# Attention norm and gated conv FFN on one core: the norm factor of batches 6 and 7 spread by transfers through DRAM, three additions made by accumulating transfers, and a new order list

## The chip, the core and the metric

One core of a Trainium2 chip runs the whole kernel. Five engines work side by side, each through its own queue in order: TensorE (PE, matmuls; PEld is its weight load), VectorE (DVE), ScalarE (ACT), GpSimd (POOL) and SyncE (SP). SP does no arithmetic here; it issues transfers. Work on one engine waits for another by semaphores. The metric is device microseconds (us) of one launch, the median of several runs; lower is better.

## The reference

```python
kv  = einsum('bhsd,bhse->bhde', k, v)            # 8 batches, 8 heads, 576 rows, head size 64
out = einsum('bhsd,bhde->bhse', q, kv)
rms = sqrt(mean(out * out, axis=-1, keepdims=True) + 1e-06)
x   = (out / rms * g_norm)  -> (8, 576, 512)     # heads side by side
h   = maximum(x @ w_in, 0.0)                     # 512 -> 1024
conv = conv_w[0] * h[s-1] + conv_w[1] * h[s] + conv_w[2] * h[s+1]
y   = (h * sigmoid(conv)) @ w_out                # 1024 -> 512
```

Inputs and the output are float32; the kernel computes with bfloat16 operands and float32 sums.

## The kernel before

Features stand on the 128 partitions and sequence positions along the free axis. A batch's 512 features of x are four blocks `t` of 128 (two heads each); `u` is a pair of blocks, `s` one of two parts of the 576 positions (320 and 256 wide for batches 6 and 7, 256 and 320 for batch 0, 288 and 288 else). The 1024 features of h are eight blocks `f`, taken in four pairs `j`.

**The order is a list.** `ORDER` is a text of 852 tokens. A token such as `sp.6.1.1.6@6` calls the function `sp` with the arguments 6, 1, 1, 6; what stands behind `@` are buffer numbers (a PSUM bank, a slot of a ring). The program is issued in this order, and a loop at the end binds each engine's instructions to it. So the list fixes what each engine does one after the other, and a token that waits holds everything behind it on its own engine, and nothing on another engine unless that needs its result.

**The steps of a batch**, by token: `Lq`, `Lk`, `Lv` (L347) load from DRAM on POOL's queue with a cast. `kv` or `kz` (L402, L479) form the 64x64 products of k and v, `kva` or `kvd` copy them out of PSUM on ACT (L416) or DVE (L414). `qt` (L433) with `qd`, or a transposing transfer `tq` (L467), turn q. `ot` or `ox` (L460, L500) make the attention output in PSUM; `sq` (L509) squares it on ACT. Batches 0 to 3 then sum the squares over a head with `on` or `oq` (L528, L537), take the factor with `nl` (L545) and scale with `mo` (L556). Batches 4 and 5, and batches 6 and 7, are normed two at a time:

- `oc` (L521, ACT) copies the attention output out of PSUM in float32.
- `ss` (L566, PE) sums the squares of both batches into one PSUM tile of 128 rows, 32 per block `t`, one row per head, part and batch; it needs all `sq` of the batch.
- `ln` (L574, ACT) takes the reciprocal root, in float32. It needs a table load on ACT when sigmoids ran before.
- `sl` (L581 to L584, DVE, four instructions) splits that tile into bfloat16 parts.
- `sp` (L593, PE, two matmuls) spreads the rows of one batch, `u` and `s` over the 64 partitions of each head, into PSUM. There are eight for a pair of batches.
- `mu` (L599, DVE) multiplies: output copy by g_norm by the spread factor, into x.

Then `hm` or `hs` (L613, L628, PE) multiply x by w_in, and `re` or `rh` (L619, L640, ACT) take the positive part into h. `hs` of part `s` needs the `mu` of both `u` of that part. For a pair `j` of features, `ta` (L681, L682, DVE, two scalings, twice) writes the two outer taps, `aa` (L687, DVE) adds them, `ab` (L692, DVE) adds h, `sg` (L698, ACT) takes the sigmoid in place, and `mg` (L722, DVE) multiplies h by it. Batches 2 to 5 do this for two batches in one instruction (2304 elements), the others for one. Two tap buffers are used in turn.

`om` (L732, PE) multiplies h by w_out, 128 rows of a pair of batches at a time, in two halves of four matmuls; `ea` (L738, ACT) or `ed` (L743, DVE) copies the 128x512 result into a ring of rows, and `st` (L748, SP) stores it. `fi` (L286) are matmuls on zeros.

Of the kernel before, what the change touches and what calls it, by code (L numbers as in the profile page):

```python
# [54 lines left out]
AL = mybir.AluOpType  # L55
# [9 lines left out]
sq.0.1.1@3 oq.0.0.1@0 nl.0.0.1@2 fi.1.512@4 fi.1.512@4 hk.0.1.0.0@4 hk.0.1.0.1 rp.1.0@0 on.0.1.1@0 nl.0.1.1@3
hk.0.2.0.0@5 hk.0.2.0.1 rp.2.0 dg.3 mo.0.0.1 dg.2 hk.0.3.0.0@4 hk.0.3.0.1 hk.0.0.0.0@2 hk.0.0.0.1 rp.0.0 hk.0.0.1.0@3
rp.3.0 hk.0.1.1.0@5 hk.0.3.1.0@0 mo.0.1.1 hk.0.3.1.1 rp.3.1 hk.0.1.1.1 rp.1.1 hk.0.0.1.1 rp.0.1 dg.0 hk.0.2.1.0@1
hk.0.2.1.1 qt.1.0.0@6 kv.1.0.1@4 rp.2.1 cv.0.2@2 sc.0.2@0 cv.0.3@0 qd.1.0.0@2 kvd.1.0.1@1 ot.1.0.1@6 sc.0.3 pl
sq.1.0.1@4 cv.0.1@4 cv.0.0@2 Lq.1.2.2 Lk.1.2.2 Lv.1.2.2 sc.0.1@1 fi.2.512@0 qt.1.1.0@0 qd.1.1.0@3 mg.0.1.1 Lo.0.8
sc.0.0 mg.0.1.0 oq.1.0.1@4 nl.1.0.1@4 mo.1.0.1@1 fi.1.512@2 hk.0.5.1.0@2 hk.0.5.0.0@3 hk.0.5.0.1 rp.5.0 hk.0.5.1.1  # L70
rp.5.1 ta.0.1.5@0 hk.0.4.1.0@0 hk.0.4.1.1 rp.4.1 hk.0.7.0.0@1 hk.0.7.0.1 kv.1.1.1@4 kvd.1.1.1 rp.7.0 ot.1.0.0@2
sq.1.0.0@5 hk.0.7.1.0@6 hk.0.7.1.1 rp.7.1 ta.0.1.7@1 ot.1.1.1@0 sq.1.1.1@6 oq.1.0.0@4 nl.1.0.0@5 mo.1.0.0 hk.0.4.0.0@6
hk.0.4.0.1 rp.4.0 hk.0.6.1.0@7 hk.0.6.1.1 rp.6.1 oq.1.1.1@4 nl.1.1.1@6 mo.1.1.1 hk.0.6.0.0@6 Lq.2.0.4@2 hk.0.6.0.1
rp.6.0 ta.0.1.4 hk.1.6.1.0@7 ta.0.1.6 hk.1.0.1.0@2 ot.1.1.0@4 sq.1.1.0@7 aa.0.1.2 hk.1.1.1.0@3 hk.1.2.1.0@6 hk.1.6.1.1
rh.1.6.1 hk.1.1.1.1 rh.1.1.1 on.1.1.0@0 nl.1.1.0@7 mo.1.1.0 hk.1.2.1.1 hk.1.5.1.0@7 hk.1.5.1.1 rh.1.5.1 rh.1.2.1
hk.1.3.1.0@3 hk.1.3.1.1 rh.1.3.1 hk.1.0.1.1 rh.1.0.1 ab.0.1.2 sg.0.1.5 sg.0.1.4 qt.2.1.0@0 qt.2.0.0@6 hk.1.5.0.0@3
hk.1.5.0.1 rh.1.5.0 qd.2.0.0@4 hk.1.0.0.0@2 hk.1.4.1.0@4 hk.1.4.1.1 hk.1.0.0.1 hk.1.1.0.0@5 hk.1.6.0.0@6 hk.1.1.0.1
hk.1.2.0.0@7 hk.1.2.0.1 rh.1.2.0 rh.1.1.0 rh.1.0.0 hk.1.6.0.1 rh.1.6.0 aa.0.1.3 qd.2.1.0@0 ab.0.1.3 sg.0.1.7 sg.0.1.6
hk.1.7.0.0@0 mg.0.1.2 hk.1.7.1.0@1 hk.1.7.1.1 rh.1.7.1 hk.1.7.0.1 rh.1.7.0 ta.1.1.1@0 ta.1.1.0 Lk.2.0.4@1 Lv.2.0.4@0
Lq.3.0.4@0 Lk.3.0.4@0 Lv.3.0.4@1 Lq.4.0.4@1 aa.1.1.0 hk.1.4.0.0@3 om.0.1.0.4@2 rh.1.4.1 hk.1.4.0.1 rh.1.4.0  # L80
om.0.2.0.4@5 kv.2.0.2@6 mg.0.1.3 om.0.1.4.4 ab.1.1.0 sg.1.1.0 sg.1.1.1 kvd.2.0.2@2 ot.2.0.1@0 sq.2.0.1@0 ed.0.1@0
st.0.1 qt.3.1.0@6 qd.3.1.0@1 Lk.4.0.4@1 Lv.4.0.4@0 Lq.5.0.4@2 om.0.2.4.4 on.2.0.1@2 qt.3.0.0@6 qd.3.0.0@2 nl.2.0.1@8
mo.2.0.1@2 om.0.3.0.4@4 ea.0.2@1 ot.2.1.1@6 ot.2.1.0@2 mg.1.1.0 om.0.3.4.4 ed.0.3@2 sq.2.1.0@1 sq.2.1.1@2 on.2.1.0@0
nl.2.1.0@9 mo.2.1.0 om.0.0.0.4@5 hk.1.3.0.0@4 on.2.1.1@0 st.0.2 nl.2.1.1@0 mo.2.1.1 om.0.0.4.4 ed.0.0@3 ot.2.0.0@2
sq.2.0.0@3 hk.1.3.0.1 rh.1.3.0 st.0.0 kv.3.0.2@0 kvd.3.0.2@0 on.2.0.0@6 nl.2.0.0@1 mo.2.0.0 hs.2.0.1@4 rh.2.0.1@1
hs.2.5.1@5 rh.2.5.1 ot.3.1.1@0 sq.3.1.1@4 ta.1.1.5@1 ot.3.0.1@6 sq.3.0.1@5 hs.2.1.1@4 rh.2.1.1 hs.2.4.0@5 rh.2.4.0
# [52 lines left out]
def kernel(  # L139
# [685 lines left out]
```

## Time and profile before

| | |
|---|---|
| median of 3 runs | 177.66 us (177.49 to 177.71) |
| the profiled execution: its span | 175.6 us |
| PE / DVE / ACT / POOL busy | 167.9 / 149.5 / 148.9 / 22.2 us |
| `om`, L732: 512-wide matmuls | 62.8 us, 267 recorded |
| input product, L628 + L658 + L613 | 34.2 + 17.7 + 16.9 us |
| `sp`, L593: 32 matmuls | 3.4 us |
| `aa` on two batches, L687: 8 | 10.9 us |
| queue q0 (POOL's loads) | 14.50 MB, 49.2% of 16 engines' time |
| queue q1 (SP, ACT) | 13.11 MB, 26.2% |

The span is from the first to the last instruction of one profiled execution; the runs are timed from outside it. Busy time is the union of an engine's instructions. Matmuls are pipelined: a row of the PE timeline gives the start of a group and the time until its last matmul ends, so what a group costs is read from its start to the start of the next one. A group's mean in the list of groups is the time of one instruction from start to end; DVE and ACT instructions of one kind overlap by a little under 0.1 us. "Landing" is the time from the issue of a transfer until its semaphore tells that the data is there.

### The profile page before, as it was taken

What the parts mean: (1) busy time and instruction counts of PE and PEld (TensorE: products, weight loads), DVE (VectorE), ACT (ScalarE), POOL (GpSimd) and SP (SyncE); (2) the same over time, 40 slices, a digit from 0 to 9 for tenths busy, and PEclk for the clock granted to TensorE, in tenths of its full rate; (3) what the DMA queues carried; (4) which work ended last, traced back from release to release, by engine and by line L of the source; (5) the groups of instructions that cost most, each with busy time, mean ns of one, the idle gap of its engine ahead of it and who ended that gap; (6) DMA issues with size and microseconds to landing.
All of it is one profiled execution on the core that took longest, in us unless ns stands there. A gap on an engine that the chain in (4) does not pass through costs nothing.

```text
span 175.6 us, 5070 instructions
## 1 busy us (share of the span) xinstructions
PE 167.9 (96%) x2097; PEld 100.0 (57%) x2114; DVE 149.5 (85%) x290; ACT 148.9 (85%) x268; POOL 22.2 (13%) x35
## 2 busy tenths in 40 slices
PE   7979999999999999999999999999999999999992
PEld 2334766676447677644467764444877744444451
DVE  2796638899688899999999998989999999999950
ACT  2368899999978999999999998999999967676721
POOL 3094512200603013030000000000000000000000
PEclk9999999999999999999999999999999999999999
DMA  5999999999999999999999050330310003064486
GB/s 159 392 323 207 207 207 207 208 208 209 207 241 230 227 207 207 170 182 197 258 181 161 14 134 0 119 123 0 119 63 0 0 0 116 13 239 175 179 304 237
DMA packets 25911, 29.11 MB, mean 166 GB/s; under 512 B 6036, under 2 KB 20384, under 8 KB 25888
## 3 DMA queue, kind: packets, MB, share of 16 engines
q0 software_dynamic: 13296, 14.50, 49.2%
q1 hardware_dynamic: 12048, 13.11, 26.2%
q10 hardware_dynamic: 544, 1.18, 1.7%
q8 instruction: 16, 0.26, 0.6%
q14 instruction: 7, 0.06, 0.1%
HBM read 32.52 MB, written 9.44 MB: 239 GB/s over the span
## 4 chain that ended last, share of the span: by engine, by line
PE 76%; DVE 12%; ACT 5%; DMA 3%; issue 3%; ACTq 0%; DVEq 0%
PE banks L732 32%; PE banks L628 14%; PE banks L613 9%; PE banks L658 4%; DMA stg<-in_v_dram 3%; PE banks L460 3%; DVE h L722 2%; PE banks L708 2%; ACT taps L698 2%; PE banks L402 2%; PE banks L593 2%; PE banks L433 1%; PE banks L528 1%; DVE taps L681 1%; PE banks L286 1%
## 5 line engine op out<-in xcount | busy, mean ns | idle before, releaser
L732 PE MATMUL banks<-w_out_sb,h 128*128 128x512 bf16 x267 | 62.8, 379 | 1.2 <-issue 0.6
L698 ACT ACTIVATE taps<-taps,cw 128x576 bf16<-128x576 bf16 (+1 forms) x44 | 40.6, 958 | 5.7 <-DVE taps L692 5.5
L732 PEld LDWEIGHTS <-h 128*128 128x128 bf16 x280 | 26.2, 98 | 30.0 <-issue 1.1
L628 PE MATMUL banks<-x,w_in_sb 128*128 128x288 bf16 (+2 forms) x256 | 34.2, 286 | 0.0
L640 ACT ACTIVATE h<-banks 128x288 bf16<-128x288 f32 (+2 forms) x80 | 29.5, 460 | 0.3 <-PE banks L658 0.2
L628 PEld LDWEIGHTS <-w_in_sb 128*128 128x128 bf16 x256 | 24.4, 98 | 7.8 <-issue 0.8
L722 DVE TENSOR_TENSOR h<-h,taps 128x1152 bf16<-128x1152 bf16 (+1 forms) x24 | 22.8, 952 | 1.2 <-ACT taps L698 1.2
L687 DVE TENSOR_TENSOR taps<-taps 128x1152 bf16<-128x1152 bf16 (+1 forms) x22 | 21.5, 978 | 0.5
L509 ACT ACTIVATE sq<-banks 128x576 bf16<-128x576 f32 (+2 forms) x32 | 20.8, 691 | 1.1 <-PE banks L460 1.1
L692 DVE TENSOR_TENSOR taps<-taps,h 128x1152 bf16<-128x1152 bf16 (+1 forms) x22 | 21.4, 972 | 0.3
L681 DVE TENSOR_SCALAR taps<-h,cw 128x576 bf16<-128x576 bf16 (+1 forms) x44 | 18.7, 424 | 0.6 <-ACT h L665 0.5
L682 DVE TENSOR_SCALAR taps<-h,cw 128x576 bf16<-128x576 bf16 (+1 forms) x44 | 18.4, 418 | 0.0
L738 ACT ACTIVATE row<-banks 128x512 f32<-128x512 f32 x23 | 13.5, 597 | 5.7 <-PE banks L732 4.2
L658 PE MATMUL banks<-x,w_in_sb 128*128 128x288 bf16 (+2 forms) x128 | 17.7, 286 | 0.1
L613 PE MATMUL banks<-x,w_in_sb 128*128 128x288 bf16 x128 | 16.9, 286 | 0.0
L556 DVE SCALAR_TENSOR_TENSOR x<-banks,cw,rs 128x576 bf16<-128x576 f32 (+2 forms) x16 | 13.0, 816 | 3.9 <-ACT rs L545 3.6
L658 PEld LDWEIGHTS <-w_in_sb 128*128 128x128 bf16 x128 | 12.0, 98 | 4.4 <-issue 0.5
L227 ACT ACT_TABLE_LOAD x10 | 12.8, 1283 | 2.0 <-issue 1.8
L613 PEld LDWEIGHTS <-w_in_sb 128*128 128x128 bf16 x128 | 12.3, 98 | 3.7 <-issue 0.2
L443 DVE COPY qT<-banks 128x1152 bf16<-128x1152 bf16 (+2 forms) x13 | 8.8, 681 | 5.7 <-PE banks L433 5.7
L545 ACT ACTIVATE rs<-banks,eps_sb 128x576 f32<-128x576 f32 (+2 forms) x16 | 11.8, 740 | 1.1 <-PE banks L528 1.1
L599 DVE SCALAR_TENSOR_TENSOR x<-o,cw,banks 128x576 bf16<-128x576 f32 (+2 forms) x16 | 12.1, 810 | 0.7 <-PE banks L593 0.5
(89 smaller groups left out, 162.9 us busy)
## 6 DMA issues: line engine op xcount, KB each, us to landing
out_dram<-row SPq DMA_DIRECT2D x35, 256.0 KB, 2.3
q_sb<-in_q_dram POOLq DMA_DIRECT2D x6, 576.0 KB, 17.9
k_sb<-in_k_dram POOLq DMA_DIRECT2D x6, 576.0 KB, 14.5
v_sb<-in_v_dram POOLq DMA_DIRECT2D x6, 576.0 KB, 17.9
stg<-in_v_dram ACTq DMA_DIRECT2D x2, 576.0 KB, 6.2
stg<-in_k_dram SPq DMA_DIRECT2D x4, 288.0 KB, 6.9
w_in_sb<-in_moe_w_in_dram POOLq DMA_DIRECT2D x2, 512.0 KB, 9.9
w_out_sb<-in_moe_w_out_dram POOLq DMA_DIRECT2D x1, 1024.0 KB, 15.5
```

The lines of the kernel that those rows point to most:

```text
L509: nc.scalar.activation(T["sq", b, u, s], T["o", b, u, s], AX.Square)
L613: nc.tensor.matmul(ps[:, s, :HS], w_in_sb[:, t, f * P:(f + 1) * P], T["x", b][:, t, c0:c1], start=(t == 0), stop=(t == NT - 1))
L628: nc.tensor.matmul(ps, w_in_sb[:, t, f * P:(f + 1) * P], T["x", b][:, t, c0:c1], start=(t == 0), stop=(t == NT - 1))
L640: nc.scalar.activation(h, fr, AX.Relu)
L658: nc.tensor.matmul(T[at], w_in_sb[:, t, f * P:(f + 1) * P], T["x", b][:, t, c0:c1], start=(t == 0), stop=(t == NT - 1))
L681: nc.vector.tensor_scalar_mul(tap[:, 0, f % 2, :n, 8:8 + S], h[:, f], cw[:, f:f + 1])
L682: nc.vector.tensor_scalar_mul(tap[:, 1, f % 2, :n, :S], h[:, f], cw[:, 2 * NF + f:2 * NF + f + 1])
L687: nc.vector.tensor_add(tap[:, 1, :, :n, :S], tap[:, 0, :, :n, 7:7 + S], tap[:, 1, :, :n, 1:1 + S])
L692: nc.vector.tensor_add(y, y, span(b, n)[:, 2 * j:2 * j + 2])
L698: nc.scalar.activation(y, y, AX.Sigmoid, scale=cw[:, NF + f:NF + f + 1])
L722: nc.vector.tensor_mul(h, h, tap_of(b, j)[:, 1, :, :n, :S])
L732: nc.tensor.matmul(T["om", p, m], h[:, f, m * P:(m + 1) * P], w_out_sb[:, f, :], start=(f == 0), stop=(f == NF - 1))
```

## The change

1. **Norm factor of batches 6 and 7.** `sl.6` and the eight `sp.*.6` are gone. `dw.6` (one transfer on SP) stores the 128 x 320 float32 tile of `ln.6` to a DRAM scratch tensor. Eight `df` (two transfers each on SP, one for each head of a block) read one row per block back into all 64 partitions of a head, as a float32 tile in a buffer of q, k or v. `mu` reads that tile instead of PSUM. Batches 4 and 5 keep `sl` and `sp`.
2. **Three additions.** `aa.4.2.3`, `aa.4.2.0` and `aa.4.2.1` on DVE become `ad`, a transfer on POOL's queue from one tap row to the other that adds to what stands there (2 x 2 x 576 bfloat16 on each of 128 partitions). Its result stands in the other row, which `ab`, `sg` and `mg` then use; after `mg` DVE sets a column of zeros again that the sum has overwritten (four elements on each partition).
3. **A new list.** All 852 tokens are laid out anew. Apart from the two edits the counts per engine stay nearly the same: two kv copies go from DVE to ACT (`kvd` to `kva`, batches 2 and 3), one `oq` becomes `on`, seven row copies go from ACT to DVE (`ea` to `ed`: 1.0, 1.2, 1.3, 1.4, 1.8, 3.5, 3.6) and six the other way (2.8, 3.0, 3.2, 3.3, 3.4, 3.7). Buffer numbers change throughout. `on` and `oq` take one PSUM bank where both halves fit in it.

The code of it:

```diff
+    dram = pool("dram", 1, space=bass.MemoryType.DRAM)
...
+    def pair(n):
+        if 2 * n <= 512:
+            return bank()[:, :2 * n].rearrange("p (e n) -> p e n", e=2)
+        return bank2()[:, :, :n]
...
-        ps = T["on", b, u, s] = bank2()[:, :, :c1 - c0]
+        ps = T["on", b, u, s] = pair(c1 - c0)
...
     @op
+    def dw(b0):
+        T["rd", b0] = dram.tile([P, GW], FP32, name="rd")
+        nc.sync.dma_start(out=T["rd", b0], in_=T["rs", b0])
+
+    @op
+    def df(b, u, s, b0):
+        w, c = width(b, s), 2 * (b - b0) + s
+        to = T["sp", b, u, s] = ring("qkv"[(4 * (b - b0) + 2 * u + s) % 3], [P, 2, 320], FP32, "spread")[:, :, :w]
+        fr = T["rd", b0].rearrange("(t c i) w -> c i t w", t=NT, i=2)[c, :, 2 * u:2 * u + 2, :w]
+        for i in range(2):
+            nc.sync.dma_start(out=to[half(i)], in_=fr[i].unsqueeze(0).to_broadcast([D, 2, w]))
...
+    @op
+    def ad(b, n, j):
+        tap = tap_of(b, j)
+        T["y", b, j] = tap[:, 0, :, :n, 7:7 + S]
+        nc.gpsimd.dma_start(out=T["y", b, j], in_=tap[:, 1, :, :n, 1:1 + S], accum_op=AL.add)
+
+    def y_of(b, n, j):
+        if ("y", b, j) not in T:
+            T["y", b, j] = tap_of(b, j)[:, 1, :, :n, :S]
+        return T["y", b, j]
...
-        nc.vector.tensor_mul(h, h, tap_of(b, j)[:, 1, :, :n, :S])
+        nc.vector.tensor_mul(h, h, y_of(b, n, j))
+        if ADS & {(b, j)}:
+            nc.vector.memset(tap_of(b, j)[:, 0, :, :n, 7:8], 0.0)
```

The stretch of the list around the two edits, before:

```
... sq.7.1.0@7 oc.7.0.1@7 om.1.1.0.4@4 om.1.1.4.4 ss.6.6.2@5 ss.7.6.2 ln.6@0 oc.7.1.1@2 st.1.0 st.1.8 ea.1.1@4 oc.7.1.0@3
om.1.4.0.4@0 om.1.4.4.4 ea.1.4@2 om.1.7.0.4@1 ta.4.2.7@1 ta.4.2.6 aa.4.2.3 ab.4.2.3 om.1.7.4.4 ea.1.7@3 ta.4.2.5
aa.4.2.2 ab.4.2.2 sg.4.2.4 sg.4.2.5 sg.4.2.7 sl.6@1 sp.6.1.1.6@6 mu.6.1.1@0 sp.6.0.1.6@4 mu.6.0.1 sp.7.0.0.6@2
mu.7.0.0@2 st.1.2 st.0.5 om.1.5.0.4@0 om.1.5.4.4 sp.7.1.0.6@6 mu.7.1.0 sp.7.0.1.6@4 sp.7.1.1.6@2 om.1.3.0.4@1
om.1.3.4.4 ea.1.3@1 st.1.3 st.1.1 hs.7.6.0@6 rh.7.6.0@1 ...
```

and after:

```
... mg.2.2.3 ta.4.2.6 ta.4.2.4@1 om.1.2.4.4 om.1.8.4.4 kx.7@1 ed.1.2@0 sq.6.0.1@3 oc.6.0.1@3 ox.7.0.1@6 ox.7.1.1@0
ad.4.2.3 oc.7.0.0@4 sq.7.0.0@4 om.1.0.4.4 sq.7.0.1@5 oc.7.0.1@5 ox.7.1.0@2 om.1.3.0.4@6 ta.4.2.5 ed.1.8@1 sq.7.1.1@6
ss.6.6.2@4 sq.7.1.0@7 ss.7.6.2 ln.6@0 ed.1.0@2 aa.4.2.2 ab.4.2.2 om.1.3.4.4 ed.1.3@3 om.1.4.0.4@5 om.1.4.4.4
om.1.1.0.4@4 sg.4.2.5 sg.4.2.4 st.1.8 st.1.0 st.1.2 ab.4.2.3 dw.6 st.1.3 df.6.1.1.6@0 ed.1.4@0 df.6.0.1.6@0 mg.4.2.2
ta.4.2.1@1 sg.4.2.6 ta.4.2.0 oc.7.1.0@6 sg.4.2.7 mg.4.2.3 om.1.1.4.4 om.1.7.0.4@5 om.1.7.4.4 ea.1.7@1 ea.1.1@2
oc.7.1.1@7 om.1.5.0.4@6 om.1.5.4.4 mu.6.1.1@0 hm.4.3@2 ea.1.5@3 re.4.3 hm.4.2@4 om.1.6.0.4@0 re.4.2 om.1.6.4.4
df.7.1.0.6@1 mu.6.0.1 hs.6.5.1@1 hs.6.3.1@2 ta.4.2.3@0 ta.4.2.2 hs.6.7.1@3 hs.6.0.1@4 ea.1.6@4 df.7.0.0.6@1
hs.6.6.1@0 mu.7.1.0@1 mu.7.0.0 hs.6.1.1@5 hs.6.2.1@6 hs.7.2.0@7 ad.4.2.0 ab.4.2.0 ... mu.6.1.0 ... mu.6.0.0 ...
ad.4.2.1 ... mu.7.1.1 ... mg.4.2.0 ... ab.4.2.1 ...
```

The list's end, after the last gate product: before, `mg.7.1.2` is followed on PE by five halves and four whole row tiles of pair 3 and by two `oh`; after, by

```
mg.7.1.2 om.3.5.4.4 ed.3.5@1 om.3.7.4.4 ea.3.0@2 st.2.5 st.3.2 ea.3.7@0 om.3.6.0.4@2 st.3.0 om.3.6.4.4 st.3.7 st.3.5 oh.3.8.0@0
ed.3.6@2 eh.3.8.0@3 st.3.6 sh.3.8.0 om.3.4.0.4@1 om.3.4.4.4 ea.3.4@0 st.3.4 oh.3.8.1@0 eh.3.8.1@1 sh.3.8.1
```

where `oh` is half a row tile (256 wide), copied by `eh` and stored by `sh`.

More of the change, by code (lines that the diff above doesn't have):

```diff
@@ L65 @@
[L65 to L74, printed above, removed]
@@ L228, in act_table @@
                 {"rs": "abs_reciprocal_sqrt_and_small", "sig": "sigmoid_and_others"}[which])
+    ADS = {tuple(int(a) for a in tok.split("@")[0].split(".")[1::2]) for tok in ORDER.split() if tok.startswith("ad.")}
     TQ = {int(tok.split("@")[0].split(".")[1]) for tok in ORDER.split() if tok.startswith("tq.")}
@@ L286, in fi, with ff @@
             nc.tensor.matmul(ps[:, :w], zero[:, :P], zero[:, :w], start=True, stop=True)
+    @op
+    def ff(n, w):
+        ps, z = bank(), zero.bitcast(FP32)
+        for _ in range(n):
+            nc.tensor.matmul(ps[:, :w], z[:, :P], z[:, :w], start=True, stop=True)
     @op
@@ L408, in kvc @@
     def kvc(eng, b, u0, n):
-        if u0 == 0:
+        if ("kvb", b) not in T:
             T["kvb", b] = ring("kvb", [P, 2, 2 * D], BF16, "kvb")
@@ L437, in qc @@
     def qc(eng, b, u, s):
-        if s == 0:
+        if ("qT", b, u) not in T:
             T["qT", b, u] = ring("qT", [P, 2, S], BF16, "qT")
@@ L584, in sl, with h_of @@
         nc.vector.scalar_tensor_tensor(w, hi, nb[:, 0:1], r, op0=AL.mult, op1=AL.add)
+    @op
+    def dw(b0):
+        T["rd", b0] = dram.tile([P, GW], FP32, name="rd")
+        nc.sync.dma_start(out=T["rd", b0], in_=T["rs", b0])
+    @op
+    def df(b, u, s, b0):
[4 more added lines that the diff above has]
+            nc.sync.dma_start(out=to[half(i)], in_=fr[i].unsqueeze(0).to_broadcast([D, 2, w]))
+    def h_of(b, f):
+        if ("h", b // 2) not in T:
+            T["h", b // 2] = ring("h", [P, NF, 2, S], BF16, "h")
+        return T["h", b // 2][:, f, b % 2, :]
     @op
```

146 lines of the change are left out of this document (78 added, 68 removed).

## The prediction

> **What bounds the kernel now.** I read the page first, then the busy time by stretches of 20 us.
>
> ```profile
> span 175.6 us, 5070 instructions
> PE 167.9 (96%) x2097; PEld 100.0 (57%) x2114; DVE 149.5 (85%) x290; ACT 148.9 (85%) x268; POOL 22.2 (13%) x35
> PE 76%; DVE 12%; ACT 5%; DMA 3%; issue 3%; ACTq 0%; DVEq 0%
> ```
>
> ```profile
> 60.00:80.00 20.00, 19.75 (x392) 12.61 (x385) 19.64 (x36) 19.93 (x43) 3.70 (x5) 1.00 1.25 191
> ...
> 100.00:120.00 20.00, 19.70 (x138) 10.10 (x139) 18.29 (x26) 19.46 (x31) 0.00 (x0) 1.00 0.28 84
> 120.00:140.00 20.00, 19.86 (x158) 14.38 (x156) 19.55 (x28) 19.85 (x38) 0.00 (x0) 1.00 0.11 40
> ```
>
> The columns after the length are busy PE, PEld, DVE, ACT, POOL, then granted clock, DMA share and GB/s. TensorE (PE) is the bound, and VectorE (DVE) and ScalarE (ACT) are nearly as full: between 60 and 140 us all three run at 91 to almost 100%. So an edit that only frees DVE buys nothing by itself, and one that frees PE is paid only where ACT can follow. The chain of waits in the second half shows that PE runs without holes:
>
> ```profile
> 97.33 3.05 PE banks L613 x24
> ...
> 141.35 10.74 PE banks L732 x49
> ```
>
> That gives prices on the path: 0.219 us for one 512-wide matmul of the output product (L732), 0.127 for one 288-wide matmul of the input product (L613).
>
> **What leaves PE.** The eight spread products of batches 6 and 7 (L593) in the PE timeline:
>
> ```profile
> 113.96 0.68 PE L566 MATMUL banks<-sq,sel 128*32 128x320 bf16 x16
> 114.56 3.63 PE L732 MATMUL banks<-w_out_sb,h 128*128 128x512 bf16 x15
> 118.22 0.42 PE L593 MATMUL banks<-wparts,spread 32*128 32x256 bf16 x6
> 118.58 1.90 PE L732 MATMUL banks<-w_out_sb,h 128*128 128x512 bf16 x8
> 120.41 0.74 PE L593 MATMUL banks<-wparts,spread 32*128 32x320 bf16 x6
> 121.08 1.90 PE L732 MATMUL banks<-w_out_sb,h 128*128 128x512 bf16 x8
> ...
> 129.67 0.31 PE L593 MATMUL banks<-wparts,spread 32*128 32x320 bf16 x4
> 129.91 2.35 PE L628 MATMUL banks<-x,w_in_sb 128*128 128x320 bf16 x18
> ```
>
> From start to the next group's start they hold PE for 0.36 + 0.67 + 0.24 = **1.27 us**, not for sixteen full matmuls, since the short ones run side by side. That is all that PE gains; the rest of its work is the same, in another order (`on` for `oq` in one place: two 288-wide matmuls for four half ones that ran in pairs).
>
> **Where the new order can lose it.** PE is in order, and it meets ACT at the second `ss` (L566), which needs the last square of batch 7. In the new list two output tiles (16 matmuls) stand behind `ss` instead of ahead of it, and half a tile (4) ahead: 12 x 0.219 = 2.63 us less before, as much more behind. ACT ahead of that square:
>
> ```profile
> L738 ACT ACTIVATE row<-banks 128x512 f32<-128x512 f32 x23 | 13.5, 597 | 5.7 <-PE banks L732 4.2 <-issue 1.4
> L416 ACT ACTIVATE kvb<-banks 128x128 bf16<-128x128 f32 x2 | 0.6, 278 | 2.8 <-PE banks L402 2.8
> ```
>
> ```profile
> 112.26 1.68 ACT L509 ACTIVATE sq<-banks 128x512 bf16<-128x512 f32 x3
> ...
> 114.45 1.28 ACT L227 ACT_TABLE_LOAD   x1
> 115.74 0.53 ACT L574 ACTIVATE rs<-banks,eps_sb 128x320 f32<-128x320 f32 x1
> ```
>
> Four row copies go to DVE (4 x 0.597); one `oc`, the same kind of copy (0.6), and two copies of kv come in. The 256-wide kv copy on ACT is in no row; twice the 128-wide row is the top, the row itself the bottom (0.28 to 0.56), and I take 0.4: ACT has 2.39 - 0.6 - 0.8 = 0.99 us less ahead of the square. In the old run the squares ended at 113.94, as `ss` ran. So `ss` can come 0.99 us earlier if ACT stays as dense, and 2.63 if ACT loses no time at all. The end moves by that, plus the 2.63 moved behind, less 1.27: between +0.37 and -1.27. ACT stood idle for 1.8 us in this stretch, and the two kv copies fall near it:
>
> ```profile
> 42.00:60.00 18.00, 17.68 (x367) 10.90 (x368) 14.42 (x29) 16.20 (x33) 4.46 (x6) 1.00 1.19 226
> ```
>
> Half of that regained puts `ss` 1.9 us earlier and the end **0.5 to 0.6** earlier; with the small gap that PE had ahead of the first spread (the list has 16 matmuls there, one record is missing: 16 x 0.219 = 3.50 of the 3.66 us from 114.56 to 118.22) I say **0.7**.
>
> **The norm through DRAM.** After `ss`, PE has 44 matmuls of L732 and 16 of L613 before it needs batch 6's x (first `hs`): 44 x 0.219 + 16 x 0.127 = 11.7 us. In that time: table load and `ln` (ended 1.7 us after `ss` in the rows above), `dw`, two `df`, two `mu`. What a transfer takes on the SP queue:
>
> ```profile
> out_dram<-row SPq DMA_DIRECT2D x35, 256.0 KB, 2.3
> stg<-in_k_dram SPq DMA_DIRECT2D x4, 288.0 KB, 6.9
> ```
>
> `dw` is a store: 2.3. A `df` (two transfers of 64 partitions, 328 KB or less) reads DRAM; the trace has no such read on an idle queue: 6.9 is five loads at once, and the store's 2.3 the low end. I take 2.3, as the queues are nearly empty there (DMA share 0.28 and 0.11 above), plus about 0.45 to issue each half. From `ss`: 1.7 + 2.3 + 0.9 + 2.3 = 7.2 for the first, 8.1 for the second, then 1.5 for two `mu`: 9.6 of 11.7. Three row stores stand ahead of `dw` on SP and one between `dw` and the first `df`; they wait for DVE copies, which come before this in DVE's order. At 6.9 the chain takes 14.2 and PE stands for 2.5 us, and the other `df` are late behind it.
>
> DVE must be there too:
>
> ```profile
> L687 DVE TENSOR_TENSOR taps<-taps 128x2304 bf16<-128x2304 bf16 x8 | 10.9, 1361 | 0.2
> L722 DVE TENSOR_TENSOR h<-h,taps 128x2304 bf16<-128x2304 bf16 x8 | 10.8, 1353 | 1.0 <-ACT taps L698 1.0
> L681 DVE TENSOR_SCALAR taps<-h,cw 128x1152 bf16<-128x1152 bf16 x16 | 8.2, 513 | 0.0
> L743 DVE COPY row<-banks 128x512 f32<-128x512 f32 x12 | 8.2, 687 | 1.6 <-PE banks L732 1.6
> L599 DVE SCALAR_TENSOR_TENSOR x<-o,cw,banks 128x512 bf16<-128x512 f32 x4 | 2.8, 744 | 0.5 <-PE banks L593 0.5
> L582 DVE SCALAR_TENSOR_TENSOR rs<-hi,na,rs 128x320 f32<-128x320 bf16 x2 | 1.1, 552 | 0.1
> L414 DVE CAST kvb<-banks 128x256 bf16<-128x256 f32 x6 | 2.5, 422 | 0.4 <-PE banks L479 0.2
> ```
>
> ```profile
> 116.30 0.33 DVE L581 CAST hi<-rs 128x320 bf16<-128x320 f32 x1 [0.28 <-ACT rs L574]
> ...
> 118.61 4.35 DVE L599 SCALAR_TENSOR_TENSOR x<-o,cw,banks 128x512 bf16<-128x512 f32 x6 [0.45 <-PE banks L593]
> ```
>
> Ahead of the first `mu` DVE loses one tap addition, the four steps of `sl` (116.30 to 118.16) and two kv copies, 1.36 + 1.86 + 0.84 = 4.1, and gains five row copies, two gate products and four tap scalings, 3.44 + 2.71 + 2.05 = 8.2. So `mu` starts 4.1 later than 118.61 at most, less the 1.7 us that DVE idled from 100 to 120: 121.0 to 122.7, done 1.5 later, 122.5 to 124.2. PE is there at 114.56 - 1.9 + 11.7 = 124.4. Close, but met. `mu` reading SBUF instead of PSUM: the SBUF row at 320 elements (552 ns) and the PSUM row at 512 (744) lie on one line of 1 ns per element, so equal; the spread tile sits in freed q, k, v buffers.
>
> **The accumulating transfers.** Each moves 576 KB from SBUF to SBUF and replaces 1.36 us on DVE, whose relief is worth nothing directly. No row shows one. Low: POOL's issue 0.74 + the smallest landing, 1.8; high: 8.2, the shortest landing of a load on that queue.
>
> ```profile
> kvx<-kvb SPq DMA_DIRECT2D x2, 32.0 KB, 1.8
> ...
> DMA to landing us min/median/max: 8.2/17.3/22.7
> ```
>
> ```profile
> 67.96 0.74 POOL L347 DMA_DIRECT2D k_sb<-in_k_dram  x1 [2.52 <-PE banks L402]
> 68.69 0.75 POOL L347 DMA_DIRECT2D v_sb<-in_v_dram  x1
> ...
> k_sb<-in_k_dram POOLq DMA_DIRECT2D x1, 576.0 KB, 12.8
> v_sb<-in_v_dram POOLq DMA_DIRECT2D x1, 576.0 KB, 14.9
> ```
>
> These two loads landed at 80.75 and 83.6, 2.8 us apart with the engines full. So 0.74 + 1.8 + 2.8 = 5.3 is my price. Between an accumulation's last scaling and the `ab` that waits for it, DVE has, by its rows, two pairs of scalings, four copies and two additions (2.05 + 2.75 + 2.72 = 7.5); then a product, two pairs and four `mu` (1.35 + 2.05 + 2.98 = 6.4); then five `mu`, an addition and a product (3.72 + 1.36 + 1.35 = 6.4). At 5.3 all are hidden; at 8.2 they are 0.7, 1.8 and 1.8 us late, and the `mu` behind them in DVE's queue with them.
>
> [...]
>
> **The tail** is covered: the last gate product has 4.7 us less DVE work ahead (three additions, `sl`, two kv and two row copies out, 8.2; five row copies in, 3.4), and PE keeps 24 matmuls of L732 and the two half tiles, over 5 us, behind it.
>
> **Rivals.**
> - *The DRAM hop is late* (0.18). Place: DVE's queue at the first `mu`, then PE at the first `hs`. For: 64 partitions fetch one row, and reads took up to 6.9. Against: empty queues. Price 2.5 less the gain of 0.7, some of it again at the next `df`: +1.8, **179.5**. It makes the kernel slower from a landing of about 5 us (2.3 + 2.1 of cover + 0.7).
> - *The accumulations are late* (0.10). [...]
> - *ACT does not follow* (0.14): +0.37, **178.0**, the spread work is gone and nothing is won.
> - *PE follows fully* (0.14): -1.27, **176.4**.
>
> **How the numbers follow.** The sum is made against the profiled execution, 175.6 us; the median of the runs is 177.66, 2.1 more for what lies around the span, which the change leaves alone. Forecast (0.44): 177.66 - 0.7 = 176.95, by itself 176.3 to 177.5. A run tells 0.2% (0.36 us) from no change. Faster: 0.14 + 0.37 of the forecast's 0.44 = 0.51; slower: 0.18 + 0.08 + 0.06 = 0.32; same: 0.17. The range takes in full gain with a little more, and most of the late hop: 176.0 to 179.2.
>
> **What would show it.** No L593 after `ss`; `ss` 1 to 2.6 us earlier than 113.96; `df` landing within 3 us of issue and `mu` waiting for no DMA; `ab` behind each accumulation not waiting; PE without a gap over 0.3 us before the first L628 of batch 6. A DVE wait on a DMA of more than 1 us there, or DMA landings of 5 us, makes it wrong.

## The result, and the profile after

The changed kernel takes **184.56 us** (median of 5 runs, 184.38 to 185.74) against 177.69 (177.49 to 177.81) for the kernel before on the same chip: a ratio of **1.040** (95% interval 1.038 to 1.042). The prediction was 176.95, range 176.0 to 179.2: wrong in sign and outside the range. The profiled execution has a span of 184.0 us, 8.4 more than before; it is the slowest of the five (185.74, the others 184.38 to 184.71), so the rows below show about a microsecond more than the change costs.

Line numbers have moved: `hs` is now L659, `om` L776, `ss` L579, `mu` L630, `dw` L602, `df` L610, `ad` L724, `ab` L734, `ed` L787, `st` L792, `rh` L671, `kz` L492.

First the page of the changed kernel: span, busy time, and the chain that ended last by engine.

```profile
span 184.0 us, 5093 instructions
...
PE 169.6 (92%) x2096; PEld 99.3 (54%) x2096; DVE 144.4 (78%) x285; ACT 150.4 (82%) x269; POOL 26.5 (14%) x38
...
PE 52%; DMA 21%; issue 10%; DVE 7%; SPq 6%; POOL 1%; ACT 1%; DVEq 0%; ACTq 0%; POOLq 0%
```

PE is busy 1.7 us more than before, so most of the 8.4 us has not gone into work. DVE has 5.1 us less, which bought nothing. What has changed is the chain: DMA was 3% of it and is 21%, SP's own issuing is 6%.

The view of waits, longest first (who waited for whom: us in total, times, longest):

```profile
PE banks L659 <- DVE x L630: 4.1, 3, 1.8
...
DVE x L630 <- DMA spread<-rd: 4.0, 3, 2.7
...
DVE taps L734 <- DMA taps<-taps: 2.3, 3, 1.2
PE banks L776 <- DVE row L787: 2.0, 1, 2.0
DVE row L787 <- DMA out_dram<-row: 1.8, 1, 1.8
...
PE banks L492 <- DMA k_sb<-in_k_dram: 1.2, 1, 1.2
```

Read it in pairs: PE waits for DVE, DVE for a transfer. The input product (L659) waits 4.1 us for `mu`, `mu` waits for the spread rows and stands behind `ab`, which waits for the accumulations; one output tile (L776) waits 2.0 us for a row copy, which waits for a row store. Each of the three kinds of transfer that meet here holds PE somewhere. The last row, a late load of k at 85 us, belongs to this execution: of that wait the profile of e9 shows 0.6 us, that of e4 0.2, those of e2 and e11 none.

Why they are late is in the queues between 119 and 140 us (share: of 16 engines' time; last column: median us from issue to landing):

```profile
q1 hardware_dynamic: 2360, 2.72, 51.9%
q0 software_dynamic: 1044, 1.17, 33.8%
issues: line engine op xcount, KB each, median us to landing
spread<-rd SPq DMA_DIRECT2D x8, 160.0 KB, 6.8
out_dram<-row SPq DMA_DIRECT2D x5, 256.0 KB, 8.6
taps<-taps POOLq DMA_DIRECT2D x2, 576.0 KB, 10.6
spread<-rd SPq DMA_DIRECT2D x8, 128.0 KB, 5.3
```

A row store took 2.3 us before, and takes 8.6 here. This stretch, almost idle before, now moves 204 GB/s at a DMA share of 0.87 (the loading stretch from 60 to 80 us moved 191 at 1.25): one row of the view by stretches for each kernel (the columns are as in the prediction; the last two are DMA share and GB/s), before and then after:

```profile
120.00:144.00 24.00, 23.80 (x179) 16.53 (x178) 23.51 (x35) 23.17 (x44) 0.00 (x0) 1.00 0.09 33
```

```profile
120.00:144.00 24.00, 19.44 (x132) 12.71 (x131) 17.57 (x28) 17.27 (x32) 2.61 (x2) 1.00 0.87 204
```

The PE timeline shows where the holes stand (start, us, group, idle before it and its releaser):

```profile
113.83 0.67 PE L579 MATMUL banks<-sq,sel 128*32 128x320 bf16 x16
...
120.88 3.61 PE L776 MATMUL banks<-w_out_sb,h 128*128 128x512 bf16 x16 [1.96 <-DVE row L787]
...
133.01 3.31 PE L659 MATMUL banks<-x,w_in_sb 128*128 128x320 bf16 x24 [1.77 <-DVE x L630]
137.14 3.43 PE L659 MATMUL banks<-x,w_in_sb 128*128 128x320 bf16 x24 [0.82 <-DVE x L630]
140.80 2.33 PE L659 MATMUL banks<-x,w_in_sb 128*128 128x320 bf16 x16 [0.23 <-ACT h L671]
144.66 2.90 PE L659 MATMUL banks<-x,w_in_sb 128*128 128x256 bf16 x24 [1.53 <-DVE x L630]
```

The second `ss` runs at 113.83, where it stood before (113.96), so all of the loss of this execution is behind it: 1.96 + 1.77 + 0.82 + 0.23 + 1.53 = 6.3 us of waits, on top of the 2.63 us of matmuls that the new list has moved behind `ss` and less the 1.27 us of spread products: 7.7 of the 8.4 us. (In e5, e12, e13 and e14, which have the same list up to there but hardly a late load of k, `ss` comes at 112.5 to 113.1.)

### The profile page after: what moved, and what is told of

Same layout as the page of the kernel before. It is cut to its first block, busy times and chain, and to the rows that moved or that the text cites. A ratio compares the mean times of both kernels' runs of the same rounds, so it can differ in the third digit from the quotient of the medians.

```text
span 184.0 us, 5093 instructions
## 1 busy us (share of the span) xinstructions
PE 169.6 (92%) x2096; PEld 99.3 (54%) x2096; DVE 144.4 (78%) x285; ACT 150.4 (82%) x269; POOL 26.5 (14%) x38
## 3 DMA queue, kind: packets, MB, share of 16 engines
q10 hardware_dynamic: 544, 1.18, 1.7%
## 4 chain that ended last, share of the span: by engine, by line
PE 52%; DMA 21%; issue 10%; DVE 7%; SPq 6%; POOL 1%; ACT 1%; DVEq 0%; ACTq 0%; POOLq 0%
PE banks L776 22%; DMA k_sb<-in_k_dram 8%; DMA spread<-rd 8%; PE banks L644 8%; PE banks L689 7%; SPq L610 4%; DMA stg<-in_v_dram 3%; DMA rd<-rs 3%; PE banks L659 2%; PE banks L293 2%; PE banks L750 2%; DVE x L630 2%; PE banks L446 2%; PE banks L415 1%; PE banks L473 1%
## 5 line engine op out<-in xcount | busy, mean ns | idle before, releaser
L776 PE MATMUL banks<-w_out_sb,h 128*128 128x512 bf16 x280 | 64.9, 379 | 2.3 <-DVE row L787 2.0
L776 PEld LDWEIGHTS <-h 128*128 128x128 bf16 x280 | 26.3, 98 | 32.3 <-issue 4.1
L659 PE MATMUL banks<-x,w_in_sb 128*128 128x288 bf16 (+2 forms) x256 | 35.2, 286 | 4.9 <-DVE x L630 4.1
L671 ACT ACTIVATE h<-banks 128x288 bf16<-128x288 f32 (+2 forms) x80 | 30.5, 459 | 2.9 <-PE banks L659 2.7
L659 PEld LDWEIGHTS <-w_in_sb 128*128 128x128 bf16 x256 | 24.3, 98 | 14.2 <-issue 4.0
L734 DVE TENSOR_TENSOR taps<-taps,h 128x1152 bf16<-128x1152 bf16 (+1 forms) x22 | 21.4, 973 | 2.6 <-DMA taps<-taps 2.3
L522 ACT ACTIVATE sq<-banks 128x576 bf16<-128x576 f32 (+2 forms) x32 | 20.6, 678 | 1.8 <-PE banks L473 1.4
L782 ACT ACTIVATE row<-banks 128x512 f32<-128x512 f32 x22 | 12.9, 591 | 9.1 <-PE banks L776 8.0
L689 PE MATMUL banks<-x,w_in_sb 128*128 128x288 bf16 (+2 forms) x128 | 18.0, 286 | 0.0
L718 DVE TENSOR_TENSOR taps<-taps 128x1152 bf16<-128x1152 bf16 (+1 forms) x19 | 17.4, 914 | 0.4
L787 DVE COPY row<-banks 128x512 f32<-128x512 f32 x13 | 8.8, 685 | 6.7 <-PE banks L776 4.9
L293 PE MATMUL banks<-zero 128*128 128x512 bf16 x37 | 11.9, 447 | 1.2 <-DVE zero L272 1.2
```

What stands on the lines that cost most here:

```text
L522: nc.scalar.activation(T["sq", b, u, s], T["o", b, u, s], AX.Square)
L659: nc.tensor.matmul(ps, w_in_sb[:, t, f * P:(f + 1) * P], T["x", b][:, t, c0:c1], start=(t == 0), stop=(t == NT - 1))
L671: nc.scalar.activation(h, fr, AX.Relu)
L689: nc.tensor.matmul(T[at], w_in_sb[:, t, f * P:(f + 1) * P], T["x", b][:, t, c0:c1], start=(t == 0), stop=(t == NT - 1))
L718: nc.vector.tensor_add(tap[:, 1, :, :n, :S], tap[:, 0, :, :n, 7:7 + S], tap[:, 1, :, :n, 1:1 + S])
L734: nc.vector.tensor_add(y, y, span(b, n)[:, 2 * j:2 * j + 2])
```

## The experiments

Fifteen kernels, all made from the changed one. Where a text speaks of a missing left tap, `ad` is left out and `ab` and the rest work on the right tap alone, unshifted; the zeros that DVE sets after `mg` (0.06 us each) fall away with it, no other work does.

### Which part costs the time

**e1: neither kind of transfer.** `dw`, `df` and `ad` are left out; `mu` of batches 6 and 7 takes the output copy in place of the norm factor, and the left tap of three pairs is missing.

```diff
- ad.4.2.3 ad.4.2.0 ad.4.2.1 dw.6
- df.6.1.1.6@0 df.6.0.1.6@0 df.7.1.0.6@1 df.7.0.0.6@1
- df.6.1.0.6@0 df.6.0.0.6@2 df.7.1.1.6@0 df.7.0.1.6@1
...
-            x_part(b, u, s), T["o32", b, u, s], g_sb, T["sp", b, u, s], op0=AL.mult, op1=AL.mult)
+            x_part(b, u, s), T["o32", b, u, s], g_sb, T.get(("sp", b, u, s), T["o32", b, u, s]), op0=AL.mult, op1=AL.mult)
```

> The new list with both kinds of transfer left out: no dw, no df (mu multiplies by the output copy instead of the factor), no ad (three feature pairs of batches 4 and 5 lack their left tap). In the profile of the changed kernel PE stood 1.96 + 1.77 + 0.82 + 0.23 + 1.53 = 6.3 us after the sums of squares at 113.8 us, all behind DVE instructions that waited for transfers. Theory Q (the transfers crowd each other on the 16 DMA engines) and theory D (the DRAM reads alone are too many bytes): these stalls go, 184.6 - 6.3 = 178.3 us, 177.5 to 179. Theory L (the new list is slow by itself: k of batch 6 late, work moved behind the squares): 181 us or more.

**e2: no accumulations.** Only the three `ad` are left out (left tap of three pairs missing).

> Only the accumulating transfers left out (three feature pairs of batches 4 and 5 lack their left tap); dw and df stay. Q: the df land in about 3.4 us, as the four before 124 us did, the row stores in 2 to 3 instead of 5.5 to 6, and the time falls to 178.5 to 180.5 us. D: the last df still land after more than 6 us, 182 us or more.

**e3: no norm through DRAM.** Only `dw` and `df` are left out, `mu` as in e1.

> Only the DRAM hop left out (mu multiplies by the output copy instead of the factor); the three ad stay. Q: each ad lands in about 6.6 us as the first did, later ones too, the ab behind them wait by less than 1 us, 178.3 to 179.5 us; the store delay at 113 to 120 us (PE 1.96 us) stays, since only the first ad runs beside it. D: 178 us, the same as with both left out.

**e4: the additions back on DVE.** Each `ad` becomes `aa`, directly ahead of its `ab`; nothing is left out.

> The three accumulations made by DVE again (aa directly ahead of its ab), dw and df stay; the result is the reference's. Q: as without ad, plus 3 x 1.36 us on DVE, some of it in front of the mu: 179 to 181.5 us. D: 182.5 us or more.

| | us | ratio to before (95%) |
|---|---|---|
| e1, neither | 177.55 | 0.999 (0.998 to 1.001) |
| e2, norm through DRAM alone | 177.32 | 0.999 (0.997 to 1.000) |
| e3, accumulations alone | 179.68 | 1.011 (1.009 to 1.013) |
| e4, norm through DRAM, additions on DVE | 180.03 | 1.013 (1.011 to 1.015) |
| the changed kernel | 184.56 | 1.040 (1.038 to 1.042) |

Four things follow. The norm through DRAM costs nothing here by itself (e2 is not slower than e1). The list with neither transfer (e1) is worth nothing: it comes out level, not the gain that I forecast for the list. The accumulations alone cost 2.1 us, nearly all of it one wait of PE for a row (1.94 us in e3's timeline); with the norm through DRAM they cost 7.2, so some 5 us lie in the meeting of the two. And DVE has become a bound: three additions of 1.36 us put back there cost 180.03 - 177.32 = 2.7 us, where I had called their relief worth nothing (in e4 DVE is busy 33.6 of the 34 us from 110 to 144).

The queues of e2 between 119 and 140 us show what the spread rows do alone:

```profile
q1 hardware_dynamic: 3024, 3.67, 67.4%
...
spread<-rd SPq DMA_DIRECT2D x8, 160.0 KB, 4.5
out_dram<-row SPq DMA_DIRECT2D x5, 256.0 KB, 4.5
spread<-rd SPq DMA_DIRECT2D x7, 128.0 KB, 4.3
```

Even without an accumulation they land in 4.3 to 4.5 us, about twice my 2.3, and with the stores fill two thirds of the engines. The list has just enough cover for that: in e2 PE waits 0.2 us, for a row, and never for `mu`.

### Which accumulation, and which wait

**e5: another row slot.** The wait of 1.96 us is for a slot of the row ring whose store is held up.

```diff
- ed.1.4@0
+ ed.1.4@6
```

> One row copy, ed.1.4, writes another slot of the row ring (6 instead of 0), so that it no longer waits for a row store that the first accumulation holds up; nothing else is touched. In the profile of the changed kernel PE loses 1.96 us behind that copy at 120.9 us and, later, 1.77 + 0.82 + 0.23 + 1.53 us behind mu, which waits for the spread rows. If the crowd of transfers from 124 us on sets the end (theory: crowding), PE only comes to those later waits earlier: the 1.96 us wait goes, the waits behind mu grow by most of it, and the time falls by less than 0.8 us, to 183.8 to 184.6. Rival, the waits add up: the whole 1.96 us is won, 182.6. If the store was not what the copy waited for, the wait stays at 1.9 us and the time at 184.5.

183.81 us (183.66 to 184.0): the wait went, 0.75 of 1.96 us was won. PE came to `mu` earlier and waited there, 3.31 us in one place.

**e7 and e8: the first accumulation alone, the other two alone.** The `ad` tokens not named are left out, with their left taps.

> Only the first accumulation, ad.4.2.3, is kept; ad.4.2.0 and ad.4.2.1 are left out, so the left tap of two pairs of batches 4 and 5 is missing. Theory crowding, with the accumulations without any spread rows at 179.7 and neither at 177.5: the first holds the row stores ahead of the norm's store and costs the 1.9 us behind ed.1.4, and the store of the norm lands in 4.6 instead of 2.7 us; nothing is crowded after 124 us, spread rows land in 3.5 to 5 us: 179.0 to 180. Rival: the first alone makes the whole chain of the norm late, and so most of the 7 us: 182 or more.

> Only ad.4.2.0 and ad.4.2.1 are kept; ad.4.2.3 is left out, so the left tap of one pair of batches 4 and 5 is missing. Theory crowding: these two stand in the queue together with six of the eight spread rows and row stores; landings of 8 us and more stay, without the 1.9 us behind ed.1.4 and with the norm's store in 2.7 us: 180.5 to 182.5. Rival, the late start of the norm's chain behind the first accumulation is what makes the rest late: then this kernel stays within 1 us of the one without accumulations, 177.3 to 178.3.

e7: 179.18 us, as expected. e8: 182.83, above the expected range. Over e2 these are 1.9 and 5.5 us, in sum 7.4 against 7.2 for all three: two damages that roughly add up. (About 1 us of e8 is a lowered clock, see the last section; at full clock the sum is 6.2.) The first accumulation stands ahead of the norm's own store. The queues of the changed kernel, of e7 and of e2 from 109 to 117 us, in this order:

```profile
out_dram<-row SPq DMA_DIRECT2D x3, 256.0 KB, 6.0
taps<-taps POOLq DMA_DIRECT2D x1, 576.0 KB, 6.6
rd<-rs SPq DMA_DIRECT2D x1, 160.0 KB, 4.6
```

```profile
out_dram<-row SPq DMA_DIRECT2D x4, 256.0 KB, 4.9
taps<-taps POOLq DMA_DIRECT2D x1, 576.0 KB, 5.8
rd<-rs SPq DMA_DIRECT2D x1, 160.0 KB, 4.5
```

```profile
out_dram<-row SPq DMA_DIRECT2D x4, 256.0 KB, 4.2
rd<-rs SPq DMA_DIRECT2D x1, 160.0 KB, 2.7
```

The norm's store (`rd`) lands in 4.5 or 4.6 instead of 2.7 us, and so the `df` behind it come later: the first of their bytes flow at 121.0 us in e7, at 119.3 in e2 (read in slices of 0.175 us).

**e15: the first alone, with the other row slot.**

> Only the first accumulation is kept (the left tap of two pairs of batches 4 and 5 is missing), and ed.1.4 writes row slot 6. With the first accumulation alone the time was 179.18 us with one wait of 1.9 us behind ed.1.4's row. If the crowd is gone with the other two, nothing takes that wait's place: 177.2 to 177.7, the time without any accumulation. Rival: the store of the norm, which stands behind the delayed row stores and lands in 4.5 instead of 2.7 us, is late next: 178.3 to 179.0.

179.53 us (179.02 to 179.63), no gain over e7's 179.18 although PE no longer waits for a row; the rival came true, a little beyond its range. The late norm store had been covered by the row wait; without it PE waits for `mu` (0.56 and 0.73 us in its timeline). Two paths are late by the same transfer, and mending one shows the other.

**e13: row slot, and the last spread rows ahead of four row stores on SP.**

```diff
- ed.1.4@0
+ ed.1.4@6
...
- df.7.1.1.6@0 ad.4.2.1
+ df.7.1.1.6@0 df.7.0.1.6@1 ad.4.2.1
...
- st.1.4 st.1.1 st.1.7 st.1.5 df.7.0.1.6@1
+ st.1.4 st.1.1 st.1.7 st.1.5
```

> Two moves in the list, the whole computation is kept: ed.1.4 writes row slot 6, and the last pair of spread rows, df.7.0.1, is issued right behind df.7.1.1 instead of behind four row stores. With the row slot alone the time was 183.81 us, and PE's last wait behind mu (1.3 us at 142.6 us, two spread rows issued at 135.4 and 136.1 us) is for this pair. If that place in the queue adds its own wait: 182.0 to 182.7. Theory crowding: the pair moves in among the accumulations, is held there as the others are, and holds them: the 3.3 us wait before it grows by about as much, and the time is 183.2 to 184.2.

183.9 us: nothing over e5 (183.81). An earlier place in the queue for this pair wins nothing.

### What fills the engines

**e6: plain copies in place of the accumulations.** The same bytes; the left tap of three pairs is overwritten by the right one.

```diff
-        nc.gpsimd.dma_start(out=T["y", b, j], in_=tap[:, 1, :, :n, 1:1 + S], accum_op=AL.add)
+        nc.gpsimd.dma_start(out=T["y", b, j], in_=tap[:, 1, :, :n, 1:1 + S])
```

> The three accumulating transfers become plain copies of the same 576 KB over the same bytes, so the left tap of three pairs of features of batches 4 and 5 is overwritten instead of added. If adding on the way is what is slow (about 110 ns for a packet of 1.15 KB in the profile of the changed kernel, against 50 to 64 ns for the packets of the spread rows), each copy lands in about 4 us, the row stores and the spread rows beside it come back to 3 to 4 us, and the time is 178 to 180.5. Rival, bytes: 576 KB more in the same engines cost the same whatever is done with them; landings of 6 to 11 us stay and the time is 183.5 to 184.8.

182.56 us (181.85 to 182.8): between the two, with 0.5 us or more of it from a lowered clock (last section). Its queues, 109 to 117 us and then 119 to 140:

```profile
out_dram<-row SPq DMA_DIRECT2D x4, 256.0 KB, 4.4
taps<-taps POOLq DMA_DIRECT2D x1, 576.0 KB, 3.5
rd<-rs SPq DMA_DIRECT2D x1, 160.0 KB, 2.6
```

```profile
q1 hardware_dynamic: 3020, 3.67, 69.5%
q0 software_dynamic: 288, 1.18, 20.6%
...
spread<-rd SPq DMA_DIRECT2D x8, 160.0 KB, 6.9
out_dram<-row SPq DMA_DIRECT2D x5, 256.0 KB, 7.0
taps<-taps POOLq DMA_DIRECT2D x2, 576.0 KB, 8.4
```

On a quiet queue the copy lands in 3.5 us where the accumulation took 6.6, and the norm's store behind it is back at 2.6. For the same 1.2 MB the accumulations hold the engines 33.8% of the stretch, the copies 20.6%: adding on the way costs 1.6 times a copy, in pieces of 1.1 instead of 4.1 KB (1.17 MB in 1044 packets, 1.18 MB in 288); whether the adding or the smaller pieces cost it, no run tells apart. But beside the spread rows the copies come to 8.4 us and hold up all the rest as well: the bytes alone are enough for a crowd.

**e12: half the bytes in the spread rows.** The factor in bfloat16, in as many pieces; the whole computation stays, at that precision.

```diff
-        r = T["rs", b0] = ring("rs", [P, GW], FP32, "rs")
+        r = T["rs", b0] = ring("rs", [P, GW], FP32 if b0 < 6 else BF16, "rs" if b0 < 6 else "rsb")
```

(and the same type for `rd` and `spread`)

> The changed kernel with the norm factor of batches 6 and 7 in bfloat16: the store and the spread rows move half the bytes in as many pieces; the accumulations stay. If the queue's engines are held by bytes, the spread rows need half their time there and the later accumulations and rows come back to 4 to 7 us: 180 to 181.5, the price of the accumulations alone and a little more. If they are held by the pieces (a row of one block for one partition, 128 pieces a transfer), nothing changes: 183.8 to 184.8.

182.2 us (182.11 to 182.72), again a part of the way, between the two ranges. Its queues between 119 and 140 us:

```profile
q1 hardware_dynamic: 3032, 2.51, 38.7%
...
taps<-taps POOLq DMA_DIRECT2D x2, 576.0 KB, 6.7
spread<-rd SPq DMA_DIRECT2D x8, 80.0 KB, 3.6
spread<-rd SPq DMA_DIRECT2D x8, 64.0 KB, 3.3
```

As many packets as in e2 (3032 and 3024) hold the engines 38.7% of the stretch instead of 67.4%, and the accumulations land in 6.7 us instead of 10.6; so what the spread rows hold goes by their bytes and not by the number of pieces. What is left on PE is the row wait (1.99 us) and 2.07 us for the last spread rows.

**e14: half the bytes and both places of e13.**

> The same two moves and the norm factor in bfloat16 (half the bytes in the store and the spread rows); the three accumulations stay, the whole computation is kept. With half the bytes alone the time was 182.2 us, and PE had two waits: 1.99 us behind ed.1.4's row and 2.1 us behind the last pair of spread rows. With the transfers' load eased, each wait is one of place, and taking both places away takes both waits: 177.6 to 178.8, level with before. Rival: also here a wait that is removed comes back at the next transfer, as with the row slot alone (1.96 us removed, 0.75 won): 180 to 181.5.

181.78 us (181.47 to 182.81): 0.4 us won over e12, hardly clear of the spread, where two waits of 2 us (1.99 and 2.07) had been taken away; PE now waits 1.71 and 1.47 us for `mu`. That is the rival's account, as in e5 and e13, 0.3 us above its range: each wait comes back at the next transfer.

### Two ways out that did not lead out

**e9: the additions on GpSimd.** Nothing is left out, and the queue is relieved of the 1.7 MB.

```diff
-        nc.gpsimd.dma_start(out=T["y", b, j], in_=tap[:, 1, :, :n, 1:1 + S], accum_op=AL.add)
+        nc.gpsimd.tensor_add(T["y", b, j], T["y", b, j], tap[:, 1, :, :n, 1:1 + S])
```

> The three accumulating transfers become three additions of GpSimd on the same rows (2304 elements each); the whole computation is kept, and the queue is left to the spread rows and the row stores. Theory crowding: without the 1.7 MB the spread rows land in 3.4 to 4.8 us as in the kernel without accumulations, and what is left to pay is GpSimd's own time. No row shows such an addition there; from above by DVE's row it takes at least 1.36 us, and up to 7.5 us it is hidden by the cover between the last scaling and the addition that waits for it. If GpSimd and DVE work side by side: 177.3 to 178.2. Rival: GpSimd's addition slows the scalings and additions of DVE beside it, or takes over 7 us; DVE is full there, so it shows as longer DVE rows and waits for GpSimd, and the time is 179 to 182.

190.48 us, far beyond the rival. Rows of its POOL and DVE timelines, in this order:

```profile
108.89 4.17 POOL L724 TENSOR_TENSOR taps<-taps 128x2304 bf16<-128x2304 bf16 x1 [30.73 <-DVE taps L713]
127.09 5.02 POOL L724 TENSOR_TENSOR taps<-taps 128x2304 bf16<-128x2304 bf16 x1 [14.03 <-DVE taps L713]
135.19 4.54 POOL L724 TENSOR_TENSOR taps<-taps 128x2304 bf16<-128x2304 bf16 x1 [3.07 <-DVE taps L713]
```

```profile
109.08 4.29 DVE L713 TENSOR_SCALAR taps<-h,cw 128x1152 bf16<-128x1152 bf16 x1
...
126.86 1.36 DVE L764 TENSOR_TENSOR h<-h,taps 128x2304 bf16<-128x2304 bf16 x1
...
128.34 4.99 DVE L630 SCALAR_TENSOR_TENSOR x<-o,cw,spread 128x512 bf16<-128x512 f32 x2
...
134.97 5.45 DVE L630 SCALAR_TENSOR_TENSOR x<-o,cw,spread 128x640 bf16<-128x640 f32 x2
```

A scaling of 0.51 us that began beside GpSimd's addition took 4.29 and ended just behind it (113.4 against 113.1); two `mu` of 0.75 us took 4.99 and ended at 133.3, the addition at 132.1, as if both had begun behind it. Two wider `mu` (1.68 us for both in e2) took 5.45 and ended at 140.4, the third addition at 139.7. So beside additions of 4.17 to 5.02 us these DVE instructions took 3.5 to 3.8 us longer than elsewhere; a gate product that ran into the second addition (126.86 to 128.22) took its usual 1.36. Part of the 190.48 us is a lowered clock as well (0.80 on average between 140 and 148 us).

**e10: e9 with a load moved; e11: e2 with the same.** `Lq.7.0.4` goes behind `Lk.6.0.4`, since the products of batch 6 wait for k.

> As the kernel with GpSimd's additions, and the load of q of batch 7 moved behind the loads of v and k of batch 6 in GpSimd's queue; the whole computation is kept. In the changed kernel k of batch 6 lands at 85.1 us, 4.3 us later than before, and the first products of that batch hold PE for 1.2 us at 85 us. If that load is what holds PE there: k lands some 2 us earlier, that wait goes, and the time is 0.8 to 1.4 us below that of the kernel with GpSimd's additions. If PE's gain is eaten at the squares on ACT, as the first theory of the list had it: within 0.4 us of it.

> The kernel without accumulations (the left tap of three pairs of batches 4 and 5 is missing), with the load of q of batch 7 moved behind those of v and k of batch 6. It tells what the new list could be worth if neither transfer cost anything. If the late load of k is what eats the list's gain: 176.0 to 176.6, 0.7 to 1.4 us less than 177.3. If ACT eats it at the squares: 177.0 to 177.6.

e10: 190.94 us (189.7 to 192.04), not to be told from e9. e11: 177.64 (176.8 to 178.18) against e2's 177.32: nothing won either, though the second `ss` came at 112.52 instead of 112.93. So the late load was not what ate the list's gain: in e11's profiled execution the 0.4 us went in waits of PE for a row, for `mu` and for ACT behind `ss` (0.43, 0.17 and 0.24 us). Ahead of `ss` ACT is full: in e2 it idles 0.34 us in the 13 us before. That fits the rival "ACT does not follow", but no run here takes work off ACT, and none has the new list with the spread products and all additions as they were, so what holds the list stays argued.

No version here beats the kernel before.

## Why the prediction was wrong

- **The step that failed** is the price of the transfers, each taken from a row of a quiet queue and each by itself: "I take 2.3, as the queues are nearly empty there (DMA share 0.28 and 0.11 above)". Those shares are of the kernel before; the change itself brings about 2.4 MB of spread rows (eight halves of 160 KB and eight of 128) and 1.2 MB of accumulations into that stretch, and the share becomes 0.87. Measured: `df` 3.4 us for the first four halves, 4.3 to 4.5 alone (medians of e2), 6.8 to 8.3 in the crowd (issued from 126 us on); `ad` 5.8 to 6.7 by itself (my price 5.3, my upper bound 8.2), 10.6 in the crowd, outside the bound. To issue a half took 0.60 us in the median and up to 1.65 in the crowd, not 0.45.
- **Store ahead on SP.** Of the row stores ahead of `dw` I wrote: "they wait for DVE copies, which come before this in DVE's order". It was their landing that mattered, 6.0 instead of 2.3 us (3.1 in e1, 4.2 in e2): it held the row ring, and the norm's store landed late with them (4.6 instead of 2.3). So transfers that were only issued delayed what landed behind them.
- **Cover.** 11.7 us for the chain and 7.5, 6.4 and 6.4 us for the accumulations were counted one beside the other, as if the transfers were independent. In e2 the cover for the norm does hold, but with 0.4 us to spare and not 2.1: from the end of `ss` to the end of the second `mu` it took 11.4 us (113.54 to 124.96) instead of 9.6, and PE was there after 11.8 (125.37). That it held alone was partly luck.
- **`ss` and ACT.** Without accumulations `ss` came at 112.93, 1.03 us earlier than before, at the lower bound that I had worked out (0.99), not at the 1.9 I chose; in the profiled execution of the changed kernel only 0.13, behind the late load of k (1.2 us of PE). That fits an ACT as dense as before, which regained none of its idle time. The list's 0.7 us did not come: e1 and e2 are level with before. The rival "ACT does not follow" had this part right.
- **"Worth nothing directly"** for DVE's relief was not true of the new list: 2.7 us by e4. For the list before, no run tells.
- **Signs.** "A DVE wait on a DMA of more than 1 us there, or DMA landings of 5 us, makes it wrong" came true: 2.69 us in front of `mu`. The two rivals on the slow side were both there (the hop late, which I had at 179.5, and the accumulations late), but as alternatives; the case in which one makes the other was not among them.
- **What held:** `mu` from SBUF costs what it cost from PSUM (0.75 us at 512 elements), and DVE in e2 is at the first `mu` at 122.82, just past the late end of the forecast's 121.0 to 122.7 (in the changed kernel, behind the row wait, at 125.2).
- **Late accumulations.** The chance of 0.10, of which 0.08 stands in the sum for slower, was my estimate; no run shows it. What the runs showed is landings of 5.8 to 6.7 us by itself and 10.6 in the crowd, and an issue of 1.30 to 1.56 us where the price has 0.74; plain copies at the same places were issued in 0.75 to 0.76 (e6), so most of the longer issue belongs to the accumulation.

## What to carry to other kernels

An idle stretch of the transfer engines is no property of the place: before a transfer is priced from a quiet row, add up the bytes that the change itself puts into the same stretch, and price the stores and reads that share it as late too. When a shared resource is the cause, taking one wait away shows little (0.75 of 1.96 us here); take the load away, one kind at a time and both together, and see whether the costs add up. An addition moved off a full engine is only free if what carries it has room: as a transfer it landed in 5.8 to 6.7 us by itself and in 10.6 in the crowd, on GpSimd it took 4.17 to 5.02 us and made DVE's scaling and `mu` beside it 3.5 to 3.8 us longer (e9).

## What was not expected of the hardware

- An accumulating transfer from SBUF to SBUF (576 KB) took 5.8 to 6.7 us on a quiet queue, a plain copy of the same rows 3.5; the engines' time for it was 1.6 times as much.
- In the SP timeline of the changed kernel nine halves of spread rows are issued in 6.01 us, 0.67 each, some 146 KB on average: about 220 GB/s (worked out). These reads and the row stores alone fill e2's engines to two thirds (67.4% between 119 and 140 us).
- In e6 and e8 PE stood still for 2.8 and 3.3 us, and the granted clock fell: in e6 to 0.88 in the stretch of the gap (128 to 132 us) and to 0.69 in the next one, in e8 to 0.57 behind the gap. The view of e8 by stretches:

```profile
132.00:136.00 4.00, 0.82 (x6) 0.60 (x7) 3.38 (x4) 2.43 (x3) 0.00 (x0) 1.00 1.14 273
136.00:140.00 4.00, 4.00 (x20) 2.36 (x18) 3.95 (x8) 3.26 (x10) 0.00 (x0) 0.57 0.85 286
```

PE worked all of the second stretch at a granted clock of 0.57. Runs of e8 with a mean clock of 1.00 and of 0.99 differ by 1.1 us (one at 181.7, the others 182.8 to 183.0), those of e6 by 0.5 to 0.95 (one at 181.85, the others 182.3 to 182.8), so e6 and e8 hold that much of a second effect; at full clock e8 lies in its expected range. In e5 the same gap of 3.31 us left the clock at 1.00 in the profiled execution; two other runs of e5 have a mean clock of 0.99 and take hardly more time for it (183.76 and 184.0 against 183.66 and 183.87). Why the clock fell with one gap of 3.3 us and not with another, and with one of 2.8 us in e6, no run here shows.
